# Second products of a two-layer expert block taken three steps behind the first, and the fill units of the attention stage reordered over more PSUM banks

## The chip, the cores and the metric

The kernel runs on one core of a Trainium2 chip. The metric is the device time of one execution in microseconds (us). The engines are TensorE (PE, matmuls), VectorE (DVE), ScalarE (ACT), GpSimd (POOL) and SyncE (SP, which here issues every DMA). Each engine works through its own queue in order and waits for the others by semaphores.

## What is computed

The reference is an attention with a decay bias, followed by two feed-forward layers; the output of each is the input of the next:

```python
scores = q @ k.T / sqrt(64) + min(bias(s), 0), causal       # 4 x 8 heads, 576 rows
x = softmax(scores) @ v                                      # 2304 tokens x 512
h = x @ w1_in;  g = max(0.01 * h, h);  x = g @ w1_out        # 512 -> 2048 -> 512
h = x @ w2_in;  g = max(h, 0) + log1p(exp(-abs(h)))          # 512 -> 2048 -> 512
return g @ w2_out                                            # 2304 x 512, float32
```

Inputs are float32 (the weights of the layers arrive as 64-bit words).

## The kernel before

All matmuls of the two layers are made of three: each operand is split into a high part and a low part (xh and xl of the tokens, gh and gl of the hidden values, wih and wil, woh and wol of the weights), and high x high, high x low and low x high are summed in PSUM. A high part comes from an ACT copy, a low part from a subtraction on POOL.

**Attention stage** (to about 278 us). For each of 16 pairs of heads, `attention` runs four units of scores, softmax and products with v through a software pipeline of 64 + 3 iterations `n`. PSUM has eight banks: tags s0 and s1 with two each for scores, t with two for transposes, a with one, and m with one. The bank m belongs to `Fill`: in each iteration `fill.step(n)` puts one *fill unit* between the attention's instructions. A fill unit is a piece of the first layer for a batch whose attention is done: either `h` (12 matmuls of 288 columns: 128 hidden rows for half a batch, then on ACT a Prelu into gf and a copy into gh, then gl on POOL) or `o` (12 matmuls of 288 columns: 128 of the 512 outputs, from the four gh and gl of that half, then an ACT copy into o and a DMA to `part`). Only the first four (`G = 4`) of the 16 hidden blocks are done this way and for three of the four batches: `ready(b)` queues, for each half of a batch, four `h` and four `o`, 48 units in all. `run` takes one unit, and takes none where an `o` lacks one of its gh and gl. What is queued after the last iteration is run by a loop behind the attention.

**Layer stage** (from about 307 us to the end). `groups` are 2 layers x 4 groups of four hidden blocks. In a group the tokens go by in five chunks (four of 512 columns and one of 256, in the middle; the very first group has only the last batch, as two chunks of 288), and for each chunk the four blocks f = 0 to 3 follow each other. Each such (chunk, f) is a *step*: 8 in the first group, 20 in each of the other seven, 148 in all; steps 0 to 67 are layer 0, steps 68 to 147 layer 1. A step `n` does `h_mm` (12 matmuls into one of three banks `ps_h`), then `tick()`, which issues what earlier steps have put off with `later`, then `act1`, which starts the activation, then weight loads and splits that a table (`plan`) gives this step, and then `out_mm(n - 2)`: 12 matmuls (6 for the chunk of 256 in layer 1) that add gh and gl of step n - 2 times the output weights into `outs`, up to four of the five banks `ps_o`. Where f is 3, `out_mm` also queues the four additions of `outs` into the running sum `acc` (DVE, line 675; ACT copies in the first group of a layer). PE's order is therefore h(n), out(n-2), h(n+1), out(n-1), and so on.

In layer 1 the activation is a loop through ACT and DVE. `act1(n)` puts Abs, Exp and Ln on ACT (lines 630 to 632). The next step's `tick` runs `act2(n)`: four DVE instructions (lines 641 to 644, the last writes gf and is the last reader of the bank `ps_h`) and `g_parts`: gh on ACT (line 147), gl on POOL (line 148). So ACT's queue reads Abs, Exp, Ln of step n, gh of step n, Abs, Exp, Ln of step n + 1: ACT waits at gh(n) for gf(n), and only then begins step n + 1.

```python
        tick()
        act1(n, layer, N, ps)
        for fn, w in sorted(plan.pop(n, ()), key=lambda x: x[0] is load_w):
            fn(*w)
        if n >= 2:
            out_mm(n - 2)
```

The split of a weight block (`split_w`) is two ACT instructions at its own step, three DVE (lines 109, 112, 115) and one POOL at the next tick, and one ACT (line 122) and one POOL (line 128) at the tick behind that. A group has eight of them. At the end of layer 0 `split_x` makes the next layer's xh and xl of a chunk: four ACT copies and four POOL subtractions, put off by one tick from the chunk's last `out_mm`.

Of the kernel before, what the change touches and what calls it, by code (L numbers as in the profile page):

```python
# [9 lines left out]
F32 = mybir.dt.float32  # L10
# [3 lines left out]
AF = mybir.ActivationFunctionType  # L14
ALU = mybir.AluOpType
# [15 lines left out]
def attn_moe_moe(ctx, tc, q, k, v, s, w1i, w1o, w2i, w2o, out):  # L31
# [139 lines left out]
    def attention(att, ps, fills):  # L171
# [274 lines left out]
        for n in range(len(units) + 3):  # L446
            p, i = divmod(n, len(order))
            u0, u1, u2, u3 = (live.get(n - d) for d in range(4))
            start(n + 1)
            if u0:  # L450
                u0.maxima(0)
                u0.exps(0)
            if u1:
                u1.divisors()
                u1.norm(0)
            if u2:
                u2.transpose(0)
            if u3:
                u3.evacuate(1)
            if i == 0:  # L460
                prep(p + 1, "q")
                load(p + 2, "q")
                rows(p + 1, bb_d)
            elif i == 2:
                prep(p + 1, "l")
                load(p + 2, "l")
            tick()
            fill.step(n)
            if u0:
                u0.maxima(1)  # L470
                u0.exps(1)
            if u1:
                u1.norm(1)
            if u2:
                u2.evacuate(0)
                u2.transpose(1)
            if i == 1:
                prep(p + 1, "k")
                load(p + 2, "k")
            elif i == 3 and p + 1 < NP:  # L480
                load(p + 1, "v")
            elif i in (0, 2) and p:
                pv(p - 1, i == 0)
            tick()


    class Fill:
        def __init__(self, ps):
            self.ps = ps
            self.units = []  # L490
            new = lambda nm, bufs=1: self.stack.enter_context(pool(nm, bufs, side="right"))
            self.stack = ExitStack()
            wio["i"] = new("rawi")
            with_o = pool("rawo", 2, side="right")
            wio["o"] = with_o.__enter__()

            blocks = [(f, nm) for nm in "io" for f in range(G)] + [(G + f, nm) for f in range(2) for nm in "io"]
            self.loads = dict(zip((0, 2, 5, 8, 11, 15, 20, 25, 30, 35, 40, 45), zip(blocks, "ioooo" + "i" * 7)))

            def begin():  # L500

                with_o.__exit__(None, None, None)
                self.gpool, self.tpool = new("gpoolA", G), new("tpoolA", 2)

            self.begin = begin

        def step(self, n):
# [6 lines left out]
                split_w(0, *self.loads[n - 3][0], (1, 2, 3, 4, 5, 6))  # L514
            self.run()

        def run(self):
            if self.units:
                fn, args = self.units[0]
                fs, nm = ([args[0]], "i") if fn == self.h else (range(G), "o")  # L520
                if fn == self.o and len(args[2]) < G or any(len(wt.get((0, f, nm), ())) < 2 for f in fs):
                    return
                self.units.pop(0)
                fn(*args)

        def ready(self, b):
            for ch in range(2):
                c0 = b * S + ch * CW
                x = xh[:, :, c0:c0 + CW], xl[:, :, c0:c0 + CW]
                gs = {}  # L530
                self.units += [(self.h, (f, x, gs)) for f in range(G)]
                self.units += [(self.o, (dm, 2 * b + ch, gs)) for dm in range(KD)]

        def h(self, f, x, gs):
            ps = self.ps.tile([P, 512], F32, tag="m", name="ps_h", bufs=1)[:, :CW]
            h_mm(ps, 0, f, *x)
            new = lambda pool, nm, dt=F32: pool.tile([P, CW], dt, tag=nm, name=nm)

            def leaky():
                gf = new(self.tpool, "gf")  # L540
                nc.scalar.activation(gf, ps, AF.Prelu, alpha=0.01)  # L541
                later(1, high, gf)

            def high(gf):
                gh = new(self.gpool, "gh", F32R)
                nc.scalar.activation(gh, gf, AF.Copy)
                later(1, low, gf, gh)

            def low(gf, gh):
                gl = new(self.gpool, "gl", F32R)  # L550
                nc.gpsimd.tensor_tensor(gl, gf, gh.bitcast(F32), op=ALU.subtract)
                gs[f] = gh, gl

            later(1, leaky)

        def o(self, dm, c, gs):
            ps = self.ps.tile([P, 512], F32, tag="m", name="ps_o", bufs=1)[:, :CW]
            w = slice(dm * P, (dm + 1) * P)
            for f in range(G):
                (wh, wl), (gh, gl) = wt[0, f, "o"], gs[f]  # L560
                for n, (a, b) in enumerate(((wh, gh), (wh, gl), (wl, gh))):
                    nc.tensor.matmul(ps, a[:, w], b, start=f == 0 and n == 0, stop=f == G - 1 and n == 2)  # L562

            def store():
                o = self.tpool.tile([P, CW], F32, tag="o", name="o")
                nc.scalar.activation(o, ps, AF.Copy)
                nc.sync.dma_start(part[c, :, dm, :], o)

            later(1, store)
# [42 lines left out]
    def split_x(c):  # L612
        for kk in range(KD):
            src = acc[:, kk, c]
            nc.scalar.activation(xh[:, kk, c], src, AF.Copy)
            nc.gpsimd.tensor_tensor(xl[:, kk, c], src, xh[:, kk, c].bitcast(F32), op=ALU.subtract)

    gs = {}

    def act1(n, layer, N, ps):  # L620

        h = ps[:, :N]
        new = lambda nm: tpool.tile([P, 512], F32, tag=nm, name=nm)[:, :N]
        t = new("t")
        if layer == 0:
            nc.scalar.activation(t, h, AF.Copy, scale=0.01)  # L626
            later(1, act2, n, layer, N, h, t, None, None)
        else:
            e, l = new("e"), new("l")
            nc.scalar.activation(e, h, AF.Abs)  # L630
            nc.scalar.activation(e, e, AF.Exp, scale=-1.0)  # L631
            nc.scalar.activation(l, e, AF.Ln, bias=1.0)
            later(1, act2, n, layer, N, h, t, e, l)

    def act2(n, layer, N, h, t, e, l):
        gf = tpool.tile([P, 512], F32, tag="gf", name="gf")[:, :N]
        if layer == 0:
            nc.vector.tensor_tensor(gf, t, h, op=ALU.max)  # L638
        else:

            nc.vector.tensor_scalar(t, e, 1.0, -1.0, op0=ALU.add, op1=ALU.add)  # L641
            nc.vector.tensor_tensor(t, l, t, op=ALU.subtract)  # L642
            nc.vector.tensor_tensor(t, t, e, op=ALU.add)  # L643
            nc.vector.scalar_tensor_tensor(gf, h, 0.0, t, op0=ALU.max, op1=ALU.add)  # L644
        gs[n] = g_parts(gpool, gf, N, 512)

    outs = {}
# [50 lines left out]
    for n, (layer, g, c, is_first, is_last, f) in enumerate(steps):  # L698
# [5 lines left out]
        act1(n, layer, N, ps)  # L704
        for fn, w in sorted(plan.pop(n, ()), key=lambda x: x[0] is load_w):
            fn(*w)
        if n >= 2:
            out_mm(n - 2)
    tick()
    out_mm(len(steps) - 2)  # L710
    tick()
    out_mm(len(steps) - 1)
    flush()


# [22 lines left out]
```

## Time and profile before

| what | value |
|---|---|
| time, median of 3 runs | 1063.96 us (1063.84 to 1065.72) |
| the profiled execution: its own time | 1065.02 us |
| its span from first to last instruction | 1063.2 us |
| mean granted TensorE clock | 0.994 of full speed |
| PE busy | 1018.3 us (96%) in 5632 matmuls |
| DVE, ACT, POOL busy | 619.7 us (58%), 544.6 us (51%), 494.2 us (46%) |

The busy share of PE is over the whole span; it says nothing of what ends a wait in one stage. The views below are the waits (who waited for whom), the timeline (instructions in order of time; a bracket gives the idle time before the instruction and what ended it), the windows (busy time of each engine in a stretch) and the chain that ended last.

### The profile page before, as it was taken

To read this page: it belongs to the slowest core of one execution; us is meant where nothing else is said; L and a number is where in the kernel's file an instruction comes from. 1 tells how busy PE (TensorE), PEld (TensorE's weight loads), DVE (VectorE), ACT (ScalarE), POOL (GpSimd) and SP (SyncE) were. 2 spreads that over 40 slices of the span, in tenths; PEclk is the share of its full clock that TensorE was granted. 3 is DMA by queue.
4 is the path that set the end of the run, shared out by engine and by line. 5 is a ranking of instruction groups with operands and counts; after the bars stand their busy time and mean duration, and the time that the engine had idled before them with its cause. 6 is when DMAs were issued, how large, how long until landed. Compare 5 with 4: busy or idle time off the path is not lost.

```text
span 1063.2 us, 15816 instructions
## 1 busy us (share of the span) xinstructions
PE 1018.3 (96%) x5632; PEld 831.6 (78%) x5632; DVE 619.7 (58%) x1325; ACT 544.6 (51%) x1167; POOL 494.2 (46%) x512
## 2 busy tenths in 40 slices
PE   6899999999889999999999998999999989999998
PEld 3667788888789888888888886788777868787886
DVE  5886756655104342433344358666886787678655
ACT  2777667665326332433344344666555545555442
POOL 5665544543225543643466666444643454335221
PEclk9999999999999999999999999999999999999999
DMA  4543433321043101200121012001210120010202
GB/s 112 130 106 79 104 89 94 82 66 35 23 155 104 57 20 41 80 31 10 40 80 40 1 40 79 21 21 40 80 40 1 40 79 23 19 40 20 80 20 80
DMA packets 89070, 61.20 MB, mean 58 GB/s; under 512 B 59616, under 2 KB 82656, under 8 KB 88960
## 3 DMA queue, kind: packets, MB, share of 16 engines
q1 hardware_dynamic: 88992, 60.19, 19.1%
q8 instruction: 45, 0.74, 0.3%
q14 instruction: 33, 0.27, 0.1%
HBM read 51.60 MB, written 8.55 MB: 57 GB/s over the span
## 4 chain that ended last, share of the span: by engine, by line
PE 58%; DVE 22%; ACT 10%; issue 5%; POOL 3%; DMA 0%; SPq 0%; POOLq 0%; DVEq 0%; ACTq 0%
PE ps_h L141 24%; PE ps_out L664 19%; DVE t L642 4%; PE ps_o L562 4%; DVE wm L115 3%; PE pt_v L386 3%; DVE t L643 3%; PE pt_s L294 3%; DVE gf L644 3%; PE pt_t L355 2%; DVE acc L675 2%; ACT gh L147 2%; ACT sc L327 2%; ACT e L631 2%; DVE t L641 1%
## 5 line engine op out<-in xcount | busy, mean ns | idle before, releaser
L148 POOL TENSOR_TENSOR gl<-gf,gh 128x512 fp32r<-128x512 f32 (+2 forms) x148 | 178.1, 1205 | 354.0 <-ACT gh L147 340.2
L141 PE MATMUL ps_h<-xh,wih 128*128 128x512 f32 (+2 forms) x688 | 247.6, 360 | 3.3 <-ACT gf L541 2.2
L141 PE MATMUL ps_h<-xl,wih 128*128 128x512 f32 (+2 forms) x688 | 245.2, 356 | 0.0
L141 PE MATMUL ps_h<-xh,wil 128*128 128x512 f32 (+2 forms) x688 | 243.9, 355 | 0.0
L147 ACT ACTIVATE gh<-gf 128x512 fp32r<-128x512 f32 (+2 forms) x148 | 85.9, 580 | 200.2 <-DVE gf L644 149.2
L141 PEld LDWEIGHTS ps_h<-xh,wih 128*128 128x128 f32 x688 | 129.8, 189 | 25.1 <-ACT gf L541 3.1
L141 PEld LDWEIGHTS ps_h<-xl,wih 128*128 128x128 f32 x688 | 129.8, 189 | 19.0
L338 POOL TENSOR_SCALAR sc<-sc,st 128x512 f32<-128x512 f32 (+4 forms) x160 | 87.7, 559 | 122.5 <-DVE st L334 45.9
L141 PEld LDWEIGHTS ps_h<-xh,wil 128*128 128x128 f32 x688 | 129.8, 189 | 18.7
L638 DVE TENSOR_TENSOR gf<-t,ps_h 128x512 f32<-128x512 f32 (+2 forms) x68 | 41.5, 610 | 170.3 <-ACT t L626 162.7
L664 PE MATMUL ps_out<-woh,gh 128*128 128x512 f32 x288 | 116.9, 406 | 10.6 <-ACT gh L147 10.6
L664 PE MATMUL ps_out<-woh,gl 128*128 128x512 f32 x288 | 117.3, 407 | 4.1 <-POOL gl L148 4.0
L327 ACT ACTIVATE sc<-sc,st 128x512 f32<-128x512 f32 (+2 forms) x144 | 83.3, 581 | 63.8 <-DVE st L313 30.9
L664 PE MATMUL ps_out<-wol,gh 128*128 128x512 f32 x288 | 115.8, 402 | 0.0
L675 DVE TENSOR_TENSOR acc<-ps_out,acc 128x512 f32<-128x512 f32 (+1 forms) x114 | 72.1, 658 | 58.8 <-PE ps_out L664 58.2
L626 ACT ACTIVATE t<-ps_h 128x512 f32<-128x512 f32 (+2 forms) x68 | 36.6, 538 | 128.3 <-PE ps_h L141 126.0
L664 PE MATMUL ps_out<-gl,woh 128*128 128x512 f32 (+2 forms) x272 | 99.3, 365 | 0.1
L664 PE MATMUL ps_out<-gh,wol 128*128 128x512 f32 (+2 forms) x272 | 99.3, 365 | 0.0
L664 PE MATMUL ps_out<-gh,woh 128*128 128x512 f32 (+2 forms) x272 | 99.0, 364 | 0.0
L118 POOL TENSOR_TENSOR wm<-wm,wt 128x512 int32<-128x512 int32 x64 | 85.7, 1341 | 22.6 <-DVE wm L115 22.0
L641 DVE TENSOR_SCALAR t<-e 128x512 f32<-128x512 f32 (+1 forms) x80 | 41.5, 519 | 85.2 <-ACT e L631 85.2
L313 DVE CUSTOM_DVE_ANT_0 sc<-pt_s,mask 128x512 f32<-128x512 f32 (+2 forms) x144 | 66.5, 480 | 39.0 <-PE pt_t L355 23.6
(105 smaller groups left out, 1871.5 us busy)
## 6 DMA issues: line engine op xcount, KB each, us to landing
rawi<-in_moe_w_in SPq DMA_DIRECT2D x32, 512.0 KB
rawo<-in_moe_w_out SPq DMA_DIRECT2D x32, 512.0 KB
out<-acc SPq DMA_DIRECT2D x18, 256.0 KB
rawq<-in_q SPq DMA_DIRECT2D x32, 128.0 KB
rawk<-in_k SPq DMA_DIRECT2D x32, 128.0 KB
V<-in_v SPq DMA_DIRECT2D x32, 128.0 KB
part<-o SPq DMA_DIRECT2D x24, 144.0 KB
acc<-part SPq DMA_DIRECT2D x6, 576.0 KB
```

The costliest lines, as they stand in the source:

```text
L118: nc.gpsimd.tensor_tensor(m, m, t, op=ALU.add)
L141: nc.tensor.matmul(ps, a, b, start=n == 0, stop=n == 3 * KD - 1)
L147: nc.scalar.activation(gh, gf, AF.Copy)
L148: nc.gpsimd.tensor_tensor(gl, gf, gh.bitcast(F32), op=ALU.subtract)
L313: nc.vector.tensor_tensor_reduce(out=self.sc[:, j, c], in0=self.ps[j][:, c], in1=m, scale=-scale, scalar=3.0e38, op0=ALU.add, op1=ALU.min, ...
L327: nc.scalar.activation(x, x, AF.Exp, scale=-1.0, bias=self.stat(0, e), accum_out=self.stat(1, e))
L338: nc.gpsimd.tensor_scalar(x, x, self.stat(2, e), 1.0, op0=ALU.mult, op1=ALU.mult)
L562: nc.tensor.matmul(ps, a[:, w], b, start=f == 0 and n == 0, stop=f == G - 1 and n == 2)
L641: nc.vector.tensor_scalar(t, e, 1.0, -1.0, op0=ALU.add, op1=ALU.add)
L642: nc.vector.tensor_tensor(t, l, t, op=ALU.subtract)
L664: nc.tensor.matmul(ps, a, b, start=f == 0 and m == 0, stop=f == G - 1 and m == 2)
L675: nc.vector.tensor_tensor(d, o, d, op=ALU.add)
```

## The change

There are four edits. In the fill units, `ready` queues a batch's units in the order h h h h h, o o o o, h h h, o o o o (the fifth h is the first of the batch's second half), and the pool of gh and gl gets a fifth buffer. From iteration 64 on, when no scores are left to compute, units rotate over m, s0 and s1 (five banks in all), and a second unit is run at the end of each iteration. In the layer stage `out_mm` is called three steps behind `h_mm` instead of two. And in layer 0 the activation is one ACT Prelu from PSUM into gf, with gh and gl at the next tick; the ACT copy times 0.01 and the DVE maximum are gone. The activation of layer 1 has the same instructions as before.

```diff
@@ in attention, iteration n
             tick()
+            if n == len(units):
+                fill.free = [("m", 1), ("s0", 2), ("s1", 2)]
             fill.step(n)
...
+            if n >= len(units):
+                fill.run()
             tick()
@@ in Fill
-                self.gpool, self.tpool = new("gpoolA", G), new("tpoolA", 2)
+                self.gpool, self.tpool = new("gpoolA", G + 1), new("tpoolA", 2)
...
+        def bank(self, nm):
+
+            tag, bufs = ("m", 1) if not self.free else self.free.pop(0)
+            if self.free is not None:
+                self.free.append((tag, bufs))
+            return self.ps.tile([P, 512], F32, tag=tag, name=nm, bufs=bufs)[:, :CW]
...
         def ready(self, b):
+            hs, os = [], []
             for ch in range(2):
...
-                self.units += [(self.h, (f, x, gs)) for f in range(G)]
-                self.units += [(self.o, (dm, 2 * b + ch, gs)) for dm in range(KD)]
+                hs += [(self.h, (f, x, gs)) for f in range(G)]
+                os += [(self.o, (dm, 2 * b + ch, gs)) for dm in range(KD)]
+
+            self.units += hs[:G + 1] + os[:KD] + hs[G + 1:] + os[KD:]
...
-            ps = self.ps.tile([P, 512], F32, tag="m", name="ps_h", bufs=1)[:, :CW]
+            ps = self.bank("ps_h")
@@ the layer stage
+    LAG = 3
...
         if layer == 0:
-            nc.scalar.activation(t, h, AF.Copy, scale=0.01)
-            later(1, act2, n, layer, N, h, t, None, None)
+            gf = new("gf")
+            nc.scalar.activation(gf, h, AF.Prelu, alpha=0.01)
+            later(1, parts, n, gf, N)
...
-        if layer == 0:
-            nc.vector.tensor_tensor(gf, t, h, op=ALU.max)
...
+    def parts(n, gf, N):
         gs[n] = g_parts(gpool, gf, N, 512)
...
-        if n >= 2:
-            out_mm(n - 2)
-    tick()
-    out_mm(len(steps) - 2)
-    tick()
-    out_mm(len(steps) - 1)
+        if n >= LAG:
+            out_mm(n - LAG)
+    for n in range(len(steps) - LAG, len(steps)):
+        tick()
+        out_mm(n)
     flush()
```

Three places show how instructions move. The first is ACT's queue at the end of the attention stage, from the last copy of attention output into xh (128x384) to the first activation of the layer stage. Each fill unit of kind o is one copy into o, each of kind h a Prelu into gf and a copy into gh. Before:

```order
L393 ACTIVATE xh<-pt_v 128x384
L566 ACTIVATE o<-ps_o 128x288 x4
L541 ACTIVATE gf<-ps_h 128x288
L546 ACTIVATE gh<-gf 128x288
...
L566 ACTIVATE o<-ps_o 128x288 x4
L626 ACTIVATE t<-ps_h 128x288
```

And in the changed kernel:

```order
L582 ACTIVATE o<-ps_o 128x288 x3
L393 ACTIVATE xh<-pt_v 128x384
L582 ACTIVATE o<-ps_o 128x288
L557 ACTIVATE gf<-ps_h 128x288
L562 ACTIVATE gh<-gf 128x288
...
L582 ACTIVATE o<-ps_o 128x288 x4
L644 ACTIVATE gf<-ps_h 128x288
```

Behind the last attention output stood twelve units (four o, four h, four o); now eight stand there (one o, three h, four o), and three o stand ahead of it.

The second place is DVE's queue in layer 1 around step 109 (the third group of that layer), from gf of step 108 to the next gf. Lines 109, 112 and 115 are the split of a weight block, line 675 (694 in the changed kernel) the four additions into acc. Before:

```order
L644 SCALAR_TENSOR_TENSOR gf<-ps_h,t 128x512
L109 TENSOR_SCALAR wm<-wm 128x512
L112 TENSOR_SCALAR wm<-wm 128x512
L115 SCALAR_TENSOR_TENSOR wm<-rawo,wm 128x512
L675 TENSOR_TENSOR acc<-ps_out,acc 128x512 x4
L641 TENSOR_SCALAR t<-e 128x512
```

And in the changed kernel:

```order
L115 SCALAR_TENSOR_TENSOR wm<-rawo,wm 128x512
L657 TENSOR_SCALAR t<-e 128x512
L658 TENSOR_TENSOR t<-l,t 128x512
L659 TENSOR_TENSOR t<-t,e 128x512
L660 SCALAR_TENSOR_TENSOR gf<-ps_h,t 128x512
L694 TENSOR_TENSOR acc<-ps_out,acc 128x512 x4
L657 TENSOR_SCALAR t<-e 128x512
```

The additions stand one activation later, so behind a split with none of their own here. Over layer 1 a split and the four additions share a gap between two activations in steps 69, 97, 109, 117 and 129 before, and in steps 94, 106, 114 and 126 now.

The third place is POOL's queue at the start of layer 1 (steps 70 to 72): line 148 makes gl, line 118 and 128 belong to weight splits, line 616 (632 in the changed kernel) is `split_x` of the last chunk. Before:

```order
L616 TENSOR_TENSOR xl<-acc,xh 128x512 x4
L148 TENSOR_TENSOR gl<-gf,gh 128x512
L118 TENSOR_TENSOR wm<-wm,wt 128x512 x2
L128 TENSOR_TENSOR wol<-wm,woh 128x512
L128 TENSOR_TENSOR wil<-wm,wih 128x512
L148 TENSOR_TENSOR gl<-gf,gh 128x512 x3
```

And in the changed kernel:

```order
L118 TENSOR_TENSOR wm<-wm,wt 128x512 x2
L632 TENSOR_TENSOR xl<-acc,xh 128x512 x4
L128 TENSOR_TENSOR wol<-wm,woh 128x512
L128 TENSOR_TENSOR wil<-wm,wih 128x512
L148 TENSOR_TENSOR gl<-gf,gh 128x512 x3
```

The four subtractions stand one tick later, between the two halves of two weight splits, and the gl of the next step stands behind all of them.

## Rows read from the trace of the kernel before

**Rows 1.** Windows: stretch, busy us of each engine (instructions), granted clock, DMA share, GB/s.
```profile
278.00:307.00 29.00, 22.56 (x146) 19.67 (x146) 0.56 (x1) 7.19 (x17) 3.21 (x4) 1.00 0.11 36
307.00:640.00 333.00, 332.88 (x1656) 280.70 (x1657) 135.39 (x210) 131.81 (x247) 170.30 (x138) 1.00 0.17 54
640.00:740.00 100.00, 94.47 (x422) 76.17 (x421) 67.19 (x100) 60.65 (x112) 47.15 (x36) 0.98 0.13 43
740.00:829.00 89.00, 86.10 (x386) 69.76 (x385) 67.49 (x98) 50.57 (x92) 41.28 (x31) 0.98 0.11 36
829.00:939.00 110.00, 104.61 (x460) 84.50 (x459) 83.84 (x122) 58.82 (x106) 48.18 (x37) 0.97 0.12 39
939.00:1039.00 100.00, 99.61 (x455) 81.85 (x454) 71.87 (x110) 50.98 (x92) 35.48 (x29) 1.00 0.12 43
```

**Rows 2.** Timeline of PE: first matmuls after the attention, and of steps 0 to 2.
```profile
278.04 0.40 PE L562 MATMUL ps_o<-gh,woh 128*128 128x288 f32 x1
...
306.86 0.40 PE L141 MATMUL ps_h<-xh,wih 128*128 128x288 f32 x1 [0.55 <-ACT o L566]
...
308.55 0.29 PE L141 MATMUL ps_h<-xh,wih 128*128 128x288 f32 x1
...
310.13 0.29 PE L141 MATMUL ps_h<-xh,wih 128*128 128x288 f32 x1
```

**Rows 3.** Timeline of ACT and POOL: one fill unit of kind h behind the attention.
```profile
294.37 0.41 ACT L541 ACTIVATE gf<-ps_h 128x288 f32<-128x288 f32 x1 [1.54 <-PE ps_h L141]
...
295.38 0.80 POOL L551 TENSOR_TENSOR gl<-gf,gh 128x288 fp32r<-128x288 f32 x1 [1.63 <-ACT gh L546]
```

**Rows 4.** Waits of PE from 640 us on: us in total, times, longest.
```profile
PE ps_out L664 <- ACT gh L147: 10.6, 5, 2.9
PE ps_out L664 <- POOL gl L148: 4.0, 9, 0.6
```

**Rows 5.** Waits of ACT and DVE on PE from 640 us on.
```profile
ACT e L630 <- PE ps_h L141: 0.9, 3, 0.5
...
DVE acc L675 <- PE ps_out L664: 7.6, 4, 2.6
```

**Rows 6.** Timeline of ACT: two gh, one undisturbed turn of layer 1's loop apart.
```profile
1045.42 0.64 ACT L147 ACTIVATE gh<-gf 128x512 fp32r<-128x512 f32 x1 [4.26 <-DVE gf L644]
...
1050.14 0.63 ACT L147 ACTIVATE gh<-gf 128x512 fp32r<-128x512 f32 x1 [2.28 <-DVE gf L644]
```

**Rows 7.** Timeline of ACT and DVE: Abs of steps 68, 105, 125, 145; additions of step 105.
```profile
632.01 0.60 ACT L630 ACTIVATE e<-ps_h 128x512 f32<-128x512 f32 x1 [3.27 <-PE ps_h L141]
...
829.23 0.60 ACT L630 ACTIVATE e<-ps_h 128x512 f32<-128x512 f32 x1 [0.22 <-PE ps_h L141]
829.93 0.69 DVE L675 TENSOR_TENSOR acc<-ps_out,acc 128x512 f32<-128x512 f32 x1 [1.59 <-PE ps_out L664]
...
938.61 0.60 ACT L630 ACTIVATE e<-ps_h 128x512 f32<-128x512 f32 x1 [0.17 <-PE ps_h L141]
...
1039.23 0.60 ACT L630 ACTIVATE e<-ps_h 128x512 f32<-128x512 f32 x1 [0.51 <-PE ps_h L141]
```

**Rows 8.** Timeline of ACT and DVE: step 109, with a weight split and four additions.
```profile
853.32 0.58 ACT L630 ACTIVATE e<-ps_h 128x512 f32<-128x512 f32 x1
853.89 1.67 DVE L115 SCALAR_TENSOR_TENSOR wm<-rawo,wm 128x512 int32<-128x512 int32 x1
855.48 2.47 DVE L675 TENSOR_TENSOR acc<-ps_out,acc 128x512 f32<-128x512 f32 x4
862.13 0.58 ACT L630 ACTIVATE e<-ps_h 128x512 f32<-128x512 f32 x1
```

**Rows 9.** The chain that ended last, 620 to 720 us: start, us, what.
```profile
626.40 2.81 PE ps_out L664 x12
...
632.01 0.61 ACT e L630
...
646.28 2.08 ACT xh L615 x4
```

More of the change, by code (lines that the diff above doesn't have):

```diff
@@ L515, in step @@
             self.run()
+        def bank(self, nm):
[3 more added lines that the diff above has]
+            return self.ps.tile([P, 512], F32, tag=tag, name=nm, bufs=bufs)[:, :CW]
+        free = None
         def run(self):
@@ L556, in o @@
         def o(self, dm, c, gs):
-            ps = self.ps.tile([P, 512], F32, tag="m", name="ps_o", bufs=1)[:, :CW]
+            ps = self.bank("ps_o")
             w = slice(dm * P, (dm + 1) * P)
@@ L623, in act1 @@
         new = lambda nm: tpool.tile([P, 512], F32, tag=nm, name=nm)[:, :N]
-        t = new("t")
         if layer == 0:
-            nc.scalar.activation(t, h, AF.Copy, scale=0.01)
-            later(1, act2, n, layer, N, h, t, None, None)
+            gf = new("gf")
+            nc.scalar.activation(gf, h, AF.Prelu, alpha=0.01)
+            later(1, parts, n, gf, N)
         else:
+            t = new("t")
             e, l = new("e"), new("l")
@@ L632, in act1, with softplus @@
             nc.scalar.activation(l, e, AF.Ln, bias=1.0)
-            later(1, act2, n, layer, N, h, t, e, l)
-    def act2(n, layer, N, h, t, e, l):
+            later(1, softplus, n, N, h, t, e, l)
+    def softplus(n, N, h, t, e, l):
         gf = tpool.tile([P, 512], F32, tag="gf", name="gf")[:, :N]
-        if layer == 0:
-            nc.vector.tensor_tensor(gf, t, h, op=ALU.max)
[L639 to L644, printed above, removed]
+        nc.vector.tensor_scalar(t, e, 1.0, -1.0, op0=ALU.add, op1=ALU.add)
+        nc.vector.tensor_tensor(t, l, t, op=ALU.subtract)
+        nc.vector.tensor_tensor(t, t, e, op=ALU.add)
+        nc.vector.scalar_tensor_tensor(gf, h, 0.0, t, op0=ALU.max, op1=ALU.add)
+        parts(n, gf, N)
+    def parts(n, gf, N):
         gs[n] = g_parts(gpool, gf, N, 512)
```

## Prediction

> **What bounds the kernel now.** I read the windows first. From 307 to 640 us PE is busy in 332.88 of 333 us [rows 1]: layer 0 has no gap to win, whatever its activation costs. Gaps are in two places: behind the attention (278 to 307 us, PE 22.56 of 29) and in layer 1, from 640 us on.
>
> Behind the attention, twelve fill units take 306.86 - 278.04 = 28.8 us, 2.40 each, and the next piece of work begins with a wait for the ACT copy of the unit before [rows 2]: all share the one bank m, so PE stands still while ACT empties it. A unit of the same 12 matmuls of 288 columns with a bank of its own takes 310.13 - 308.55 = 1.58 us [rows 2].
>
> In layer 1 the view of waits names gh and gl alone, 10.6 + 4.0 us in 14 waits [rows 4]. That reads as if PE were the bound and the second product came a little too early. It is not all. The view of waits for the other side shows that the loop through ACT and DVE waits hardly ever for PE: Abs 0.9 us in three waits, the additions 7.6 us in four, one of which, 2.6 us, is the last of the kernel [rows 5]. So from 640 us on, the loop stands still for PE during 0.9 + 5.0 = 5.9 us only. Its turn is 4.72 us where nothing disturbs it [rows 6], shorter than a PE step, but the splits and additions lie in it: step 109, with a split and four additions, takes 862.13 - 853.32 = 8.8 us [rows 8]. Over 20 steps the two can be compared. From Abs of step 105 to that of step 125 it is 938.61 - 829.23 = 109.4 us [rows 7]. The next 20 steps take 100.6 us, in which PE is busy nearly throughout (99.61 of 100 us) [rows 1, 7], so 20 steps of PE work are about 100.2 us. The loop, with its waits for PE (1.59 and 0.17 us belong to the first stretch [rows 7]) taken off, needs 107.6. **The loop is the longer of the two chains**; where they touch (829.23, 938.61, 1039.23), they differ by 0.2 to 0.5 us [rows 7]. A PE that never waits for gh would still be paced by it.
>
> **The change part by part.** The sum is made against the profiled execution: 1065.0 us, of which 1.8 lie around its span of 1063.2.
>
> *The last units.* Twelve waits go: 28.8 - 12 x 1.58 = 9.8 us [rows 2]. The number of matmuls stays; four units move ahead of the last attention output and lie on PE there at the same 1.58 us, with PE nearly full, so moving them alone gives nothing. Two waits come. The last o units follow the last h directly: PE reaches the last gl after some 10 of 12 matmuls, 1.3 us, while Prelu, gh and gl take 295.38 + 0.80 - 294.37 = 1.8 us [rows 3] and begin only when the product is through: 0.5 us and a little, taken at 0.7. And step 0 needs a bank of the old pool, whose last reader may be the last ACT copy: between 0 and 0.8 us (what a unit loses now), taken at 0.4. The DMAs of o move with their units; behind them in SP's queue stand the loads of `acc` and of weights for steps 5 and on, which follow PE as before: 0. Gain 8.7 us, bounds 8.0 to 9.8.
>
> At this place a page speaks against the edit, and this can be read by itself. The Trainium skill (TensorE: Matmul & The Clock Gate, section HAM oscillation) reports a kernel for which "Adding PSUM double-buffering gave no further gain". By it this term would be 0 and the time 1056. The trace disagrees in the cause: the wait here ends with ACT's copy out of the bank, where that kernel's was for DMA.
>
> *Layer 0.* ACT has one instruction per step before and after, a read of PSUM of the same shape; DVE loses 68 maxima. All of it lies beside PE at 332.88 of 333 us [rows 1]: 0. The cover is a full step; if it went, a Prelu of 0.4 us [rows 3] or somewhat more per step would show.
>
> *Three steps behind.* The loop's instructions and their order within ACT's queue stay, so its own 107.6 us per 20 steps stay. Three things change.
> (a) The loop starts when PE reaches step 68: Abs there waits 3.27 us for PE [rows 7]. With one more `out_mm` put off, that point has one block of 12 matmuls less ahead of it: 2.8 us [rows 9]. The block is not lost, it moves behind, where PE waits anyway.
> (b) With PE further ahead of the loop, the loop's waits for PE fall away: 5.9 us at most [rows 5]. PE now may lead until the bank `ps_h` of step n is wanted by h(n+3); gf(n) then has about 14.0 us (five blocks of 2.8 [rows 9]) from the end of h(n), where gh(n) had to be there after 11.2 (four blocks). So PE keeps some 3 us more lead into each meeting point, and two of the three meetings, at 829 and 938 us, should vanish. Before the third lie 20 steps in which the loop gains 0.8 us a step where it is undisturbed; I leave 0.7 us of its 2.4. Gain 5.2, bounds 0 and 5.9.
> (c) The additions move by one step. Where they share a gap with a split, the step costs 8.8 instead of 4.7 us [rows 6, 8]; the order of DVE's queue shows five such steps before and four now. The one that goes is step 69; but `split_x`, 2.1 us on ACT [rows 9] and four POOL subtractions, now falls into the tick of two splits. I set the two against each other, 0, with bounds of a gain of 3 (the 4.1 us of the shared step without the price of a lone one) and a loss of 3 (the 2.1 us plus a late gl). The gl behind these subtractions comes some 5 us later; PE waits for it, the loop doesn't.
> Sum of the lag: 2.8 + 5.2 + 0 = 8.0 us, bounds 0 and 12.
>
> PE's waits don't vanish, they move: from gh before `out_mm` to gf (DVE) before `h_mm`, where nearly the whole queue of PE stands behind them, and the loop goes on meanwhile.
>
> *Sum.* 1065.0 - 8.7 - 8.0 = 1048.3 us. The median of the three runs is 1.1 us below the profiled execution, so the forecast for a median is 1047 us.
>
> **The rivals.**
> *PE is the bound after all.* If one step more of slack ends every wait of PE in layer 1, it saves 14.6 us of waits [rows 4] and the time at the lower clock. The granted clock was 0.98 of full speed in two windows of 100 and 89 us and 0.97 in one of 110 [rows 1], that is, partly at 1.2 instead of 2.4 GHz after the longer waits: 2.0 + 1.8 + 3.3 = 7.1 us. The time would be 1065.0 - 8.7 - 21.7 - 1.1 = 1033.5. For it: no wait of PE is longer than 2.9 us [rows 4], and a step is 5.6 (two blocks [rows 9]). Against it: 107.6 against 100.2 us per 20 steps, and ACT and DVE waiting 5.9 us in 400. Chance 0.12. The Trainium skill (Perfetto Trace Analysis, section Identifying the Most-Contended Engine) would take this side, since it takes the engine with the highest occupancy as the bottleneck; DVE and ACT are far below PE in every window. By it the time is this rival's, but a loop across two engines has no occupancy of its own.
>
> *The lag gives nothing.* The two chains touch again at the same points because the wait for the bank `ps_h` (or for an addition to free a bank of `ps_o`) holds PE back as the wait for gh did. Then only the last units pay: 1065.0 - 8.7 - 1.1 = 1055. For it: the limit of 14.0 us is only 2.8 above the old one, and the additions' limit hardly moves. Chance 0.13.
>
> *The last units stay serial*: banks handed over late by the old tags, or the two o buffers waiting for their DMA to `part`. Then 1065.0 - 8.0 - 1.1 = 1056. Against it: the order shows ACT's copies as before, and five banks in place of one. Chance 0.05.
>
> *Slower.* A step in which a split and the additions share DVE costs 8.8 - 4.7 = 4.1 us over an undisturbed turn [rows 6, 8]. If the additions, one step later, came to meet a split, or the POOL half of one, at more places than now, each would cost the loop up to that. Five more such places decide it (20.5 us against 16.7 of gain), ten give 1065.0 - 16.7 + 41 - 1.1 = 1088. The order of DVE's queue shows one place fewer, so POOL's half alone would have to do it. Chance 0.03.
>
> **How the numbers follow.** Forecast, 1043 to 1051: 0.62. PE-bound, 1030 to 1038: 0.12. Lag gives nothing, 1052 to 1056: 0.13. Units serial: 0.05. Slower: 0.03. The rest, 0.05, is a gain so small that it can't be told from none, or a mix. About 0.2% (2 us) is what the measurement can tell from no change. So faster has 0.62 + 0.12 + 0.13 + 0.05 = 0.92, same 0.04, slower 0.04. The range of 1038 to 1056 leaves out most of the PE-bound case (0.10) and what lies above (0.08); 1056 is the bound at which the lag gives nothing, 1038 the one at which two thirds of what the PE-bound case adds (13.7 us) come on top of my sum.
>
> **What would show it.** Right: the first step of the layers begins about 8.7 us earlier, the units behind the last attention output follow each other at 1.58 us. PE's waits in layer 1 stand mostly under DVE gf at line 141's `ps_h`, not under gh; their sum stays over 8 us. 20 turns of the loop in the middle take 107 to 108 us, and the waits of Abs and of the additions for PE are nearly gone. Wrong: PE's waits in layer 1 gone and 20 steps in about 100 us (PE-bound), or waits for PE in the loop as large as before (lag gives nothing), or a turn at the steps with a split and additions over 8.8 us, or a start of layer 1 that takes more than 3 us longer from Abs of step 68 to that of step 73.

## The result, and the profile after

| what | before | after |
|---|---|---|
| time, median (lowest to highest) | 1064.84 us (1063.84 to 1066.03), 4 runs | 1047.03 us (1046.71 to 1047.55), 4 runs |
| the profiled execution: time, span | 1065.02, 1063.2 us | 1046.71, 1044.9 us |

The ratio is 0.983 (95% interval 0.982 to 0.985): 17.8 us faster by the medians, 18.3 us by the profiled executions. The rows after that answer to those of before come here, the windows first (columns as in [rows 1]).

```profile
278.00:297.00 19.00, 18.11 (x137) 16.96 (x136) 1.12 (x2) 6.03 (x15) 2.40 (x3) 1.00 0.17 56
297.00:610.00 313.00, 312.81 (x1571) 264.85 (x1572) 80.16 (x130) 121.55 (x232) 156.43 (x128) 1.00 0.17 58
610.00:710.00 100.00, 96.69 (x440) 78.74 (x439) 70.05 (x96) 60.36 (x112) 54.69 (x42) 1.00 0.10 32
710.00:810.00 100.00, 97.06 (x436) 79.20 (x435) 76.34 (x110) 58.82 (x107) 45.81 (x36) 0.98 0.13 43
810.00:920.00 110.00, 106.01 (x474) 86.41 (x473) 84.78 (x125) 59.56 (x106) 48.09 (x37) 0.98 0.12 39
920.00:1020.00 100.00, 99.17 (x453) 81.25 (x452) 72.47 (x112) 51.31 (x92) 35.79 (x28) 1.00 0.12 43
```

The gap behind the attention is closed (18.11 of 19 us busy), layer 0 stays full, and layer 1 is still not. The timeline of PE shows the last product of the attention, the first matmuls of some of the eight units behind it, and the first step of the layers.

```profile
281.24 1.52 PE L386 MATMUL pt_v<-PB,V 128*64 128x128 f32 x16
282.69 0.40 PE L578 MATMUL ps_o<-gh,woh 128*128 128x288 f32 x1
284.38 0.29 PE L141 MATMUL ps_h<-xh,wih 128*128 128x288 f32 x1
...
289.19 0.30 PE L578 MATMUL ps_o<-gh,woh 128*128 128x288 f32 x1
...
291.31 0.40 PE L578 MATMUL ps_o<-gl,woh 128*128 128x288 f32 x1 [0.53 <-POOL gl L567]
...
297.19 0.40 PE L141 MATMUL ps_h<-xh,wih 128*128 128x288 f32 x1 [0.55 <-ACT o L582]
```

Three h units follow each other in 289.19 - 284.38 = 4.81 us, 1.60 each. Only two waits are left, of 0.53 and 0.55 us idle, where the prediction put them. The eight units take 297.19 - 282.69 = 14.5 us; where the twelve began, at 278.04 [rows 2], the first of eight begins 4.65 us later, with four units more ahead of it.

The views of waits from 610 us on, of PE, ACT and DVE (us in total, times, longest):

```profile
PE ps_out L683 <- DVE acc L694: 6.4, 4, 3.4
PE ps_out L683 <- ACT acc L692: 3.5, 3, 1.3
PE ps_out L683 <- POOL gl L148: 0.9, 1, 0.9
PE ps_h L141 <- DVE gf L660: 0.3, 1, 0.3
...
ACT gh L147 <- DVE gf L660: 145.5, 78, 4.9
...
ACT e L649 <- PE ps_h L141: 4.1, 2, 3.3
...
DVE acc L694 <- PE ps_out L683: 5.0, 3, 3.8
```

PE still waits 11.1 us, where 14.6 stood in [rows 4]: no longer for gh, but at the output banks `ps_o`, for the additions (DVE) and copies (ACT) that empty them. The wait at `ps_h`, where the prediction put it, is 0.3 us. The other way, ACT's 3.3 us are step 68's (as 3.27 in [rows 7]), and DVE's 3.8 are the end of the kernel.

The timeline of ACT at Abs of steps 68, 105, 125 and 145:

```profile
618.96 0.60 ACT L649 ACTIVATE e<-ps_h 128x512 f32<-128x512 f32 x1 [3.34 <-PE ps_h L141]
...
814.13 0.58 ACT L649 ACTIVATE e<-ps_h 128x512 f32<-128x512 f32 x1
...
922.01 0.58 ACT L649 ACTIVATE e<-ps_h 128x512 f32<-128x512 f32 x1
...
1020.72 0.58 ACT L649 ACTIVATE e<-ps_h 128x512 f32<-128x512 f32 x1
```

The waits for PE that stood at steps 105, 125 and 145 in [rows 7] are gone. With these rows the span can be split:

| stretch | before, us | after, us | gained |
|---|---|---|---|
| start to first step of the layers | 306.86 | 297.19 | 9.7 |
| from there to Abs of step 68 | 325.15 | 321.77 | 3.4 |
| Abs 68 to 105 | 197.22 | 195.17 | 2.0 |
| Abs 105 to 125 | 109.38 | 107.88 | 1.5 |
| Abs 125 to 145 | 100.62 | 98.71 | 1.9 |
| Abs 145 to the end of the span | 23.97 | 24.18 | -0.2 |

The last line has a cause of its own. The chain that ended last (start, us, what) shows it:

```profile
1027.23 2.73 PE ps_h L141 x12
1029.97 9.15 PE ps_out L683 x39
...
1039.14 0.69 DVE acc L694
```

Behind the last h stand four blocks of out instead of three, back to back. The 9.15 us are three of them and the first 3 matmuls of the fourth, behind which the first addition can start. The last gl is there at 1036.09 + 1.30 = 1037.39 us (timeline of POOL), the last block begins at 1038.24 (timeline of PE): here PE is the later one, and about 1 us of what the loop gained is lost.

### The profile page after: what moved, and what is told of

It reads as the page before. It is cut to its first block, busy times and chain, and to the rows that moved or that the text cites. A ratio compares the mean times of both kernels' runs of the same rounds, so it can differ in the third digit from the quotient of the medians.

```text
span 1044.9 us, 15686 instructions
## 1 busy us (share of the span) xinstructions
PE 1009.9 (97%) x5632; PEld 829.4 (79%) x5632; DVE 576.9 (55%) x1257; ACT 543.8 (52%) x1167; POOL 493.0 (47%) x512
## 4 chain that ended last, share of the span: by engine, by line
PE 59%; DVE 25%; ACT 11%; issue 2%; POOL 1%; DMA 1%; SPq 0%; DVEq 0%; ACTq 0%; POOLq 0%
PE ps_h L141 23%; PE ps_out L683 20%; DVE t L658 5%; DVE t L659 4%; DVE gf L660 4%; DVE wm L115 4%; PE ps_o L578 4%; PE pt_v L386 3%; PE pt_s L294 3%; PE pt_t L355 2%; DVE acc L694 2%; ACT gh L147 2%; ACT e L650 2%; ACT l L651 2%; DVE t L657 2%
## 5 line engine op out<-in xcount | busy, mean ns | idle before, releaser
L147 ACT ACTIVATE gh<-gf 128x512 fp32r<-128x512 f32 (+2 forms) x148 | 85.6, 579 | 146.3 <-DVE gf L660 145.5
L644 ACT ACTIVATE gf<-ps_h 128x512 f32<-128x512 f32 (+2 forms) x68 | 36.7, 540 | 175.5 <-PE ps_h L141 175.3
L109 DVE TENSOR_SCALAR wm<-wm 128x512 f32<-128x512 f32 x64 | 30.6, 477 | 168.5 <-ACT wm L103 168.5
L683 PE MATMUL ps_out<-woh,gl 128*128 128x512 f32 x288 | 114.7, 398 | 0.9 <-POOL gl L148 0.9
```

What stands on the lines that cost most here:

```text
L683: nc.tensor.matmul(ps, a, b, start=f == 0 and m == 0, stop=f == G - 1 and m == 2)
```

## The experiments

**The two halves apart.** `fill_only` has the new fill units and the old layer stage, `lag_only` the reverse.

```diff
@@ fill_only: attention and Fill as after; the layer stage keeps
         if n >= 2:
             out_mm(n - 2)
@@ lag_only: attention and Fill as before; in the layer stage
+            nc.scalar.activation(gf, h, AF.Prelu, alpha=0.01)
+            later(1, parts, n, gf, N)
...
+        if n >= LAG:
+            out_mm(n - LAG)
```

> The kernel before with the edits of the fill units alone (order of units, banks, second unit per iteration); second products stay two steps behind. Theory (the edits act in two places and add up: 9.7 us of the 18.3 come from the last units): first step of the layers 9 to 10 us earlier, time 1054 to 1055.5, layer stage as before within 1 us. Rival (the lag is what pays; a unit's wait moves to the start of the layers): under 5 us gained, 1059 or more.

> The kernel before with the edits of the layer stage alone (second products three steps behind, Prelu in layer 0). Theory (layer 1 is paced by the loop through ACT and DVE; the lag brings its start 3.4 us forward and takes its waits for PE away, 6.4 us, and gives 1.2 back at the end): 8 to 9 us faster than before, 1055 to 1056. Rival 1 (PE's waits for gh are the cost, and each one that goes is gained): 14 to 22 us faster, 1042 to 1050. Rival 2 (the lag gives nothing by itself): within 2 us of before.

Measured: `fill_only` 1054.73 us, ratio 0.991 (0.989 to 0.993), 10.3 us faster than before's 1065.0 on the same chip; its first layer step begins at 297.59 and PE's waits in layer 1 are 9.1 us for gh and 4.2 for gl, nearly as before. `lag_only` 1056.43, ratio 0.992 (0.991 to 0.994), 8.6 us faster, with PE waiting 7.5 us for DVE's additions and 3.4 for ACT's. The halves add up (10.3 + 8.6 = 18.9, together 17.8), so they pay at different places. The 8.6 us contain the Prelu of layer 0, which `prelu_only` below prices alone. No run takes away the second unit per iteration or the fifth buffer of the fill units, so their shares are not known. The rivals "the lag gives nothing" and "units stay serial" fall here.

**Is the loop the bound?** One DVE instruction of the loop is issued twice in each of the 80 steps; it gives the same value again.

```diff
         nc.vector.tensor_scalar(t, e, 1.0, -1.0, op0=ALU.add, op1=ALU.add)
+        nc.vector.tensor_scalar(t, e, 1.0, -1.0, op0=ALU.add, op1=ALU.add)
```

> The changed kernel with line 657, the first DVE instruction of layer 1's activation, issued twice: the same values, 0.48 us more on DVE in each of 64 steps and 0.28 in each of 16 (35 us in all), at a place where 0.2 us of it lie beside ACT's Ln. PE's work is the same. Theory (the loop paces layer 1): nearly all of it is lost, 20 to 35 us slower than the changed kernel, 1067 to 1082, and PE's waits grow by as much. Rival (PE is the bound, the loop only has to be in time, and gf stands ready 2 to 8 us before it is wanted): at most 5 us slower.

Measured: 1091.77 us, ratio 1.025 (1.023 to 1.026), 44.7 us above the changed kernel. The groups by line (busy us, mean ns | idle before) show the price of the addition, and the timeline of ACT 20 steps (Abs 105 and 125):

```profile
L658 DVE TENSOR_SCALAR t<-e 128x512 f32<-128x512 f32 (+1 forms) x80 | 51.5, 644 | 2.7
```
```profile
835.71 0.58 ACT L649 ACTIVATE e<-ps_h 128x512 f32<-128x512 f32 x1
...
955.26 0.58 ACT L649 ACTIVATE e<-ps_h 128x512 f32<-128x512 f32 x1
```

The added work is 51.5 us, more than the 35 expected. In 47 of the 64 full steps the added instruction took 0.41 to 0.43 us, but in 17, where a POOL instruction was already running as it began, 1.38 to 1.41 (see the last section). Of it 44.7 us, 87%, come out at the end; 20 steps take 119.55 instead of 107.88 us, 11.7 more, where 20 x 0.644 = 12.9 were added. DVE is busy 55% of the span in the changed kernel and 57% here, and yet its added work costs nearly its full length. The loop is the bound.

**Opening the loop.** In the changed kernel ACT's queue reads Abs, Exp, Ln of step n, gh(n), Abs of n + 1: Abs stands behind gh(n), which waits for DVE (145.5 us in 78 waits above). `act_first` puts Abs, Exp, Ln of step n + 1 ahead of gh(n).

```diff
-            later(1, parts, n, gf, N)
+            later(2, parts, n, gf, N)
...
-            later(1, softplus, n, N, h, t, e, l)
+            later(2, softplus, n, N, h, t, e, l)
...
-        tick()
         act1(n, layer, N, ps)
+        tick()
```

> The changed kernel with act1(n) issued ahead of tick(): ACT's queue has Abs, Exp and Ln of step n ahead of gh of step n-1, so ACT no longer waits for gf before it begins the next step. Instructions and their number are the same; gh comes about 1.9 us later after gf. Theory (the closed loop of 4.7 us a turn paces layer 1): with the loop open, PE is the bound, its waits of 11 us in layer 1 go, 1030 to 1038. Rival (PE's waits come from the time between a product and its gh, not from the rate): gh later by 1.9 us, no gain or some us lost, 1046 to 1052.

Measured: 1036.52 us, ratio 0.974 (0.972 to 0.975), 10.5 us below the changed kernel: the best version here. The views of waits of PE and ACT from 600 us on:

```profile
PE ps_out L683 <- POOL gl L148: 2.6, 1, 2.6
PE ps_out L683 <- POOL wol L128: 1.8, 1, 1.8
...
ACT e L649 <- PE ps_h L141: 135.3, 68, 3.1
ACT gh L147 <- DVE gf L660: 28.3, 18, 3.0
```

The timeline of ACT at Abs of steps 105 and 125:

```profile
808.85 0.60 ACT L649 ACTIVATE e<-ps_h 128x512 f32<-128x512 f32 x1 [3.09 <-PE ps_h L141]
...
908.76 0.60 ACT L649 ACTIVATE e<-ps_h 128x512 f32<-128x512 f32 x1 [3.06 <-PE ps_h L141]
```

And windows of layer 1:

```profile
600.00:700.00 100.00, 95.64 (x430) 78.18 (x429) 75.31 (x94) 60.66 (x112) 58.87 (x42) 0.98 0.13 43
700.00:800.00 100.00, 100.00 (x458) 82.55 (x457) 84.68 (x115) 61.63 (x113) 49.48 (x36) 1.00 0.13 43
800.00:900.00 100.00, 100.00 (x458) 82.56 (x457) 90.38 (x120) 57.77 (x104) 49.64 (x36) 1.00 0.13 43
```

The roles have changed: ACT waits for PE at 68 of 80 steps, 20 steps take 908.76 - 808.85 = 99.91 us (the prediction's estimate for PE's work was 100.2), and in both windows from 700 to 900 us PE is busy in 100.00 of 100 us. DVE is busier than in the changed kernel (622.5 us in all for 576.9, by the pages): t<-t,e, which now meets a running POOL instruction in most steps, takes 1.1 us or more in 48 of the 64 full steps, for 4 there. That no longer shows in the time. The page's part on the chain that ended last says the same, first the changed kernel, then this one:

```profile
PE 59%; DVE 25%; ACT 11%; issue 2%; POOL 1%; DMA 1%; SPq 0%; DVEq 0%; ACTq 0%; POOLq 0%
```
```profile
PE 86%; DVE 6%; ACT 4%; POOL 2%; issue 1%; DMA 0%; SPq 0%; DVEq 0%; ACTq 0%; POOLq 0%
```

The Trainium skill's rule (Perfetto Trace Analysis, section Identifying the Most-Contended Engine) is to take the engine of the highest occupancy first, where TensorE's headroom is to be judged by its rate of arithmetic or its weight loads rather than by busy matmul time. It agrees with the trace of this kernel alone. In the changed kernel PE is the busiest as well by either measure (matmuls 97%, weight loads 79%, DVE 55%), and the loop sets the time.

**Four steps behind.** First the lag alone, then with a fifth buffer for gh and gl. The second run changes two things: to make room, it also lets the scratch tile t share gf's buffer.

```diff
-    LAG = 3
+    LAG = 4
@@ lag4_bufs also
-    gpool = ctx.enter_context(pool("gpool", bufs=4, side="right"))
+    gpool = ctx.enter_context(pool("gpool", bufs=5, side="right"))
...
-        gf = tpool.tile([P, 512], F32, tag="gf", name="gf")[:, :N]
+        t = gf = tpool.tile([P, 512], F32, tag="gf", name="gf")[:, :N]
```

> The changed kernel with second products four steps behind instead of three. Theory (the loop paces layer 1 and no longer waits for PE from step 70 on, so more lead of PE is worth nothing; the start that comes one block earlier is given back at the end, where four blocks instead of three follow the last first product): within 2 us of the changed kernel, 1045 to 1049. Rival (each step of lag removes waits of PE, and they are the cost): 3 to 8 us faster, 1039 to 1044.

Measured: 1053.92 us, ratio 0.990 (0.988 to 0.991), 7 us above three steps: a miss of both theories. The view of waits of ACT from 600 us on shows a wait that no other kernel has (the pool of gh and gl has four buffers, so gh(n) needs out(n-4) to be through):

```profile
ACT gh L147 <- PE ps_out L683: 11.2, 8, 2.3
```

Beside it the additions fall on a step with two splits: from Abs of step 71 to that of 72 it is 651.36 - 638.00 = 13.4 us. Two causes, so a further run:

> Four steps behind, with a fifth buffer for gh and gl (the room comes from the scratch tile t of layer 1, which now lies in gf's own buffer; no instruction is added or taken away). With four buffers and four steps, gh(n) needs out(n-4) done, which PE reaches only right behind h(n), so the loop waited for PE at gh (11.2 us in 8 waits) and the kernel took 1053.9 us. Theory: these four buffers are what made four steps slower than three. Then gh(n) needs out(n-5), as far off as at three steps with four buffers, the loop's waits for PE at gh go, and the time is within 2 us of the changed kernel: 1045 to 1049. Rival: the additions, which now fall on steps where two splits or split_x already stand (71, 111, 131), cost the loop that time; then buffers change nothing and it stays at 1052 to 1056. In between, both have a part.

Measured: 1046.48 us, ratio 0.983 (0.981 to 0.986), the ratio of the changed kernel. The number is the theory's, but the trace does not show its cause. Three of the eight waits lie in layer 0, and the five in layer 1 (7.3 us) are no longer than the wait for gf: gh begins 0.09 us after gf's end there as in the other turns. What differs is each turn. The timelines of DVE and ACT in step 101, in the changed kernel, `lag4` and `lag4_bufs`:

```profile
797.88 0.69 DVE L659 TENSOR_TENSOR t<-t,e 128x512 f32<-128x512 f32 x1
798.68 0.69 DVE L660 SCALAR_TENSOR_TENSOR gf<-ps_h,t 128x512 f32<-128x512 f32 x1
799.41 0.63 ACT L147 ACTIVATE gh<-gf 128x512 fp32r<-128x512 f32 x1 [2.28 <-DVE gf L660]
```
```profile
804.59 0.69 DVE L659 TENSOR_TENSOR t<-t,e 128x512 f32<-128x512 f32 x1
805.39 0.69 DVE L660 SCALAR_TENSOR_TENSOR gf<-ps_h,t 128x512 f32<-128x512 f32 x1
806.17 0.63 ACT L147 ACTIVATE gh<-gf 128x512 fp32r<-128x512 f32 x1 [2.34 <-DVE gf L660]
```
```profile
799.68 0.69 DVE L658 TENSOR_TENSOR gf<-gf,e 128x512 f32<-128x512 f32 x1
800.40 0.69 DVE L659 SCALAR_TENSOR_TENSOR gf<-ps_h,gf 128x512 f32<-128x512 f32 x1
801.13 0.63 ACT L147 ACTIVATE gh<-gf 128x512 fp32r<-128x512 f32 x1 [2.21 <-DVE gf L659]
```

An undisturbed turn takes 4.73, 4.79 and 4.66 us. Two gaps make the difference. From the end of gf to gh it is 0.03 us in the changed kernel and 0.09 in `lag4`, where the trace has a semaphore instruction of its own ahead of gh in 75 of 80 steps (none in the changed kernel, 15 in `lag4_bufs`). From the end of t<-t,e to gf it is 0.10 us in both, and 0.03 in `lag4_bufs`, where t and gf are one tile and such an instruction ahead of gf is gone. Over the 80 steps the first gap sums to 4.2, 9.3 and 5.6 us, the second to 8.1, 8.0 and 2.4. From `lag4` to `lag4_bufs` the fifth buffer thus gave some 3.7 us and the shared tile some 5.6, where the time fell by 7.4. An estimate from these sums for the fifth buffer alone is 1050 to 1052 us, 3 to 5 above three steps; no run shows it. So the rival is not refuted: the turn of step 71 takes as long as in `lag4` (649.45 - 636.18 = 13.3 us, timeline of ACT).

The fourth step also gives back at the end what it gains at the start: in `lag4_bufs` the loop ends earlier (gh of the last step at 1033.15 instead of 1035.38 us), but five blocks of out are left behind the last h, not four, and the last additions wait 5.87 us for PE instead of 3.80 (timelines of ACT and DVE).

**The banks of the last units, and their order.** `one_bank` leaves out the rotation, `old_order` only the new order.

```diff
@@ one_bank
-            if n == len(units):
-                fill.free = [("m", 1), ("s0", 2), ("s1", 2)]
@@ old_order
-            self.units += hs[:G + 1] + os[:KD] + hs[G + 1:] + os[KD:]
+            self.units += hs[:G] + os[:KD] + hs[G:] + os[KD:]
```

> The changed kernel with every fill unit on bank m again, order and second unit per iteration kept. Theory (nearly the whole gain of the last units is the wait for the one bank, 0.8 us for each of the ten to twelve units that follow each other): 7 to 9.5 us slower than the changed kernel, 1054 to 1056.5. Rival (order and pairing of units do half of it): 3 to 6 us slower.

> The changed kernel with the old order of units (four h, four o, four h, four o of a batch), the banks and the second unit per iteration kept. Theory (moving units ahead of the last attention output gives nothing where PE is full; only an iteration without a unit leaves a gap of PE): 0 to 1.5 us slower than the changed kernel, 1047 to 1048.5. Rival (the order is what lets units follow each other): 3 us slower or more.

Measured: `one_bank` 1053.43 us, ratio 0.989 (0.988 to 0.991), 6.4 above the changed kernel; its layers begin at 303.88 instead of 297.19 (timeline of PE), with a wait for ACT at every one of the last eight unit boundaries. `old_order` 1048.63, ratio 0.985 (0.983 to 0.986), 1.6 above. So the banks are worth two thirds of the first term. The rest comes from the four units moved ahead: at one bank they pay 306.86 - 303.88 = 3.0 us. The first of the eight units behind begins at 284.28 there (timeline of PE), so the four in front take 284.28 - 278.04 = 6.2 us, 1.6 each, and the eight behind 303.88 - 284.28 = 19.6, 2.4 each. The Trainium skill (TensorE: Matmul & The Clock Gate, section HAM oscillation) reports of one kernel, whose waits were for DMA, that "Adding PSUM double-buffering gave no further gain". Here the waits end with ACT's copy out of the bank, and more banks gave 6.4 us.

**Other sizes.** `banks44` moves a bank from `ps_o` to `ps_h`; `act_first_lag2` is `act_first` two steps behind; `act_first_spread` is `act_first` with the four pieces of `split_x` three ticks apart; `prelu_only` is before with the Prelu alone.

```diff
@@ banks44
-    ps_h = ctx.enter_context(pool("ps_h", bufs=3, space=PSUM))
-    ps_o = ctx.enter_context(pool("ps_o", bufs=5, space=PSUM))
+    ps_h = ctx.enter_context(pool("ps_h", bufs=4, space=PSUM))
+    ps_o = ctx.enter_context(pool("ps_o", bufs=4, space=PSUM))
@@ act_first_lag2
-    LAG = 3
+    LAG = 2
@@ act_first_spread
+            later(3 * kk + 2, split_xk, c, kk)
...
-            later(1, split_x, slice(c0, c0 + N))
+            split_x(slice(c0, c0 + N))
@@ prelu_only, on before
-            nc.scalar.activation(t, h, AF.Copy, scale=0.01)
+            nc.scalar.activation(gf, h, AF.Prelu, alpha=0.01)
```

> The changed kernel with four banks for the first products and four for the second, instead of three and five. PE's waits in layer 1 stood nearly all at the banks of the second products, for additions; with four, the first of a chunk waits too. Theory (where PE waits costs nothing as long as the loop goes on): PE's waits change, the time stays within 2.5 us of the changed kernel, 1045 to 1050. Rival (those waits are the cost): 4 us slower or more.

Measured 1048.01 us, ratio 0.984 (0.983 to 0.986), 1.0 above the changed kernel. Its waits of PE move once more (4.1 us for ACT's copies, 4.0 for DVE's additions, 2.3 put down to Abs): where the loop is the bound, PE's waits change place and keep about their sum (12.1 us with gl and gh, for 11.1).

> The kernel with act1 ahead of tick (1036.5 us), with second products two steps behind instead of three. With the loop open, gh comes about 8.2 us after the end of its product and gl 9.6, against 11.2 us with a lag of two, so splits and additions make it late now and then. Theory: with the loop open it is latency that PE waits for, and here the lag pays: 4 to 9 us slower than with three, 1040 to 1046. Rival (the lag never mattered for PE): within 2 us of 1036.5.

Measured 1061.78 us, ratio 0.997 (0.996 to 0.998): 25 us above `act_first`, nearly three times the upper end expected. Its view of waits of PE, over the whole span:

```profile
PE ps_out L683 <- POOL gl L148: 19.2, 18, 2.0
...
PE ps_out L683 <- ACT gh L147: 3.4, 2, 2.3
```

With Abs ahead of gh, gh and gl come later after their h, and two steps of lag no longer cover it. The opened loop needs the third step; the closed one gains 8.6 us by it, with the Prelu. At two steps the opened loop is even 7 us slower than the closed one (`fill_only`, 1054.73, with the old activation of layer 0): the new order of ACT's queue pays only together with the lead.

> The kernel with act1 ahead of tick (1036.5 us), and the four copies and four subtractions of split_x put three ticks apart instead of all in one. The waits of PE left there are 2.6 us for gl and 1.8 for a weight at the start of layer 1, behind POOL's subtractions. Theory (they are POOL's queue): both go, 3 to 5 us faster, 1031.5 to 1033.5. Rival (they come from the two weight splits of that tick): within 1.5 us of 1036.5.

Measured 1036.86 us, ratio 0.974: no gain, a miss. PE's waits for `wol` went and those for gl fell to 0.4 us, but 3.2 us of waits for ACT's copies out of `ps_o` took their place.

> The kernel before with the Prelu of layer 0 alone. Theory (layer 0 is PE without a gap): within 1.5 us of before. Rival (DVE's maxima slow POOL or the weight splits): 2 us faster or more.

Measured 1063.26 us, ratio 0.999 (0.998 to 1.000), in ten runs: 1.7 us below before's 1064.94 on the same chip (0.3 to 2.4 us by the interval), between the two expectations. Abs of step 68 comes 0.15 us earlier (631.86); 20 turns from Abs 105 take 108.1 instead of 109.4. So the Prelu itself is hidden; why the loop's meetings shift a little is open. They shift without it too: `fill_only`, whose layer stage is that of before, takes 928.11 - 819.61 = 108.5 us for these turns.

## Why the prediction was right, point by point

*The time.* Forecast 1047, measured 1047.03. Two misses cancel in it: the profiled execution came 1.6 us below the 1048.3 of the sum (1046.71), and the median lies 0.3 us above that execution, where 1.1 us below was taken. That it is met to 0.1 us is luck; the mechanism, a loop that is longer than PE's work, is shown by `longer_loop` and `act_first`.

*The last units.* 9.7 us for 8.7, within the bounds. Two sizes are off in it. The two waits were taken at 1.1 us; their idle time is 1.08, but the eight units take 14.5 us where 8 x 1.58 = 12.6, so they cost 1.9. And "moving them alone gives nothing" is off by the 1.6 us of `old_order`: four units take 4.65 us in front, not 4 x 1.58 = 6.3. In `one_bank` the same four take 6.2, so it needs the banks too; what time they fill is not shown (PE's idle time from 78 us to the last product of the attention falls only from 4.3 to 3.5 us, windows of PE).

*Layer 0* at nothing: right, 312.81 of 313 us, and in `prelu_only` layer 1 begins only 0.15 us earlier.

*Three steps behind, (a).* 2.8 us for the block that moves behind step 68; measured 3.4 for the stretch.

*(b) and (c).* 5.2 + 0 us, measured 2.0 + 1.5 + 1.9 - 0.2 = 5.2. The parts are less exact than the sum. Waits of the loop for PE fell from 5.9 [rows 5] to 4.1 - 3.3 + 5.0 - 3.8 = 2.0 us, so (b) gave 3.9, not 5.2. What it lacks, and 1 us more for the loss at the end, is put down to the moved additions (c), taken at 0, because nothing else is left: from Abs of step 68 to that of step 73 the time falls from 37.49 to 34.83 us (timeline of ACT), and part of this is given back from step 88 to 105 (88.91 to 89.94). How much of the start is (b) and how much (c) can't be told from these rows. Nor are they good to 1 us: from Abs 68 to Abs 145 before takes 407.2 us, `fill_only`, also two steps behind, 406.1, and the changed kernel and `lag_only` 401.8 each. The end was not in the sum: one more block behind the last h.

*Where PE waits.* Wrong: not at `ps_h` for gf, but at `ps_o` for the additions. The prediction named that limit ("an addition to free a bank of `ps_o`"), only in the rival by which the lag gives nothing. The sum of the waits, which follows from the loop, was right: over 8 us. `banks44` shows that the place is not what costs.

*20 turns* in 107 to 108 us: 107.88. *PE-bound*, the rival of 1033.5: refuted by `longer_loop`. That it names what lies behind the loop is shown by `act_first`, which comes to 1036.5 once Abs no longer stands behind gh. *Slower*: the price of additions on a step with splits is real (8.6 to 8.7 us for the turns of steps 94, 106, 114 and 126, and 13.4 for step 71 in `lag4`), but such places became fewer, as the order showed.

## What to carry to other kernels

An engine at 97% busy can still be paced by two others at 52 and 55%, if these form a loop: compare the time of 20 turns, with the other work that falls into them, with that of 20 steps of the busy engine, and look which side hardly ever waits for the other. Giving more lead to the side that waits removes little more than the meetings of the two chains (8.6 us here, some 3 of them a block that moved behind the loop's start); reordering one queue so that the next turn's first instruction does not stand behind the last one's copy removes the bound (10.5 us more), but only with the longer lead. And a run that changes two things can meet its number by the wrong one: look at a single turn of the loop before and after (4.79 and 4.66 us with the fifth buffer and the shared tile).

## What the runs showed of the hardware

A DVE instruction can be held up by a POOL instruction that is already running. Of the 128x512 instructions of the loop in the changed kernel, t<-l,t (both inputs in SBUF) takes 0.69 us in 47 of 64 cases, with no POOL instruction beside it, and 1.59 to 1.61 us in 17, all of which begin while one is running. Overlap alone does not do it: t<-t,e (both inputs in SBUF) overlaps POOL in 17 cases too, and takes 1.66 to 1.67 us in the 4 where POOL began first, but 0.69 in the 13 where POOL began later. Nor does it take two SBUF inputs: t<-e, a TENSOR_SCALAR with one, takes 1.30 to 1.50 us in 6 cases, all behind a running POOL instruction, and 0.41 to 0.48 in the others. gf, with one input in PSUM and one in SBUF, takes 0.69 to 0.70 us in all 64, 18 of them beside POOL. The timelines of DVE and POOL in step 72 show one of each, three of them held up:

```profile
647.73 1.30 DVE L657 TENSOR_SCALAR t<-e 128x512 f32<-128x512 f32 x1 [1.85 <-ACT e L650]
649.14 1.59 DVE L658 TENSOR_TENSOR t<-l,t 128x512 f32<-128x512 f32 x1
650.77 1.66 DVE L659 TENSOR_TENSOR t<-t,e 128x512 f32<-128x512 f32 x1
652.53 0.69 DVE L660 SCALAR_TENSOR_TENSOR gf<-ps_h,t 128x512 f32<-128x512 f32 x1
```
```profile
648.71 1.47 POOL L128 TENSOR_TENSOR wol<-wm,woh 128x512 fp32r<-128x512 f32 x1
650.15 1.74 POOL L128 TENSOR_TENSOR wil<-wm,wih 128x512 fp32r<-128x512 f32 x1
```

The Trainium skill (SBUF — State Buffer, section Who interferes with whom) says that a DVE instruction with two SBUF inputs contends with a GpSimd instruction that reads SBUF, and one with at most one SBUF input does not, unless it runs in a mode that takes both ports, which it says TENSOR_SCALAR can. The trace agrees with all three: some 0.9 us more for t<-l,t and for t<-e, none for gf. So POOL's work is part of the loop. By these counts its part is 17 x 0.9 + 4 x 1.0 + 6 x 0.9 = 25 us of the 64 full steps, an estimate; no run takes it away.

A second semaphore to wait for costs an instruction some 0.06 us here: gh and gf begin 0.03 us after the instruction that they follow where the trace has no semaphore instruction of its own ahead of them, and 0.09 to 0.10 us where it has one (`lag4` and `lag4_bufs` above).
